# Soft shrinkage one slot sooner, and two extra frequency rows in another PSUM bank

## The chip, the cores and the metric

The kernel runs on one core of one Trainium2 chip. The time is the device time of one execution in microseconds (us), and the time of a kernel is the median over several runs. One execution of each kernel was recorded by the hardware profiler. The core's engines are PE (matrix multiply), PEld (its weight loads), DVE (vector), ACT (scalar activations), POOL (general SIMD) and SP (which issues most DMAs). They run side by side, each through its own queue in order, and wait for each other on semaphores.

## The reference

One block of a network on a single sequence of 4096 tokens with 640 features: an adaptive layer norm, a spectral mixer, another layer norm and a gated feed-forward layer.

```python
mod = (_silu(c) @ w_mod)            # six vectors of 640: sa, ca, ga, sb, cb, gb
h = _layernorm(x) * (1 + ca) + sa
x = x + ga * _A_ref(h, A_w1, A_b1, A_w2, A_b2)     # spectral mixer
h = _layernorm(x) * (1 + cb) + sb
x = x + gb * ((_silu(h @ w_gate) * (h @ w_up)) @ w_down)
```

The mixer takes a real Fourier transform over the 4096 tokens, giving 2049 complex frequencies. For each frequency the 640 features fall into 4 blocks of 160, and each block goes through a complex two-layer network: a first layer with a rectifier, a second layer with a bias. The outputs are then shrunk:

```python
lam = 0.01
mr = jnp.abs(or_) - lam
or_ = jnp.sign(or_) * mr * (mr > 0)        # the same for the imaginary part
```

An inverse transform brings the result back to tokens. Shrinking `v` is the same as `relu(v - lam) - relu(-v - lam)`, and the same as `v - clamp(v, -lam, lam)`; the kernel uses both forms.

## The kernel before

The kernel has two parts. The first does the layer norm, the forward transform, the two-layer network, the shrinkage and the first half of the inverse transform. The second finishes the inverse transform and does the feed-forward layer; its instructions are put in order by a planner that runs when the kernel is built, with estimated costs, and it knows nothing of the first part's order. In both parts the order of each engine's queue is the order of the program text; a tile framework adds the semaphore waits that the data and the buffers need.

The first part, around the change, works on 8 chunks (`ch`) of frequencies with 4 feature blocks (`b`) each, so 32 units, and runs through slots `p` from 0 to 31. `on(f, p)` calls `f(p // 4, p % 4)`. Slot p, from 4 to 28 (`LAST` is 28), emits in this order:

- `stage_l1(p)`: the first layer of unit p. Its matmuls (L727) write three PSUM tiles `pl`: two with the tag `p1`, a third (the remainder features) with the tag `p3`. ACT reads each of the first two twice (L744, L745), DVE forms a low half `h` from the results (L746), ACT and DVE read the third (L758, L759).
- `stage_b`: the forward transform of a block of the next chunk (PE L631), with its evacuation on ACT (L638) and DVE (L639).
- in some slots, sums that make the modulation vectors (a `pm` tile, with the tag `p3` in some of them), and copies of the remainder features (DVE L685).
- `tail_l1(p)`: the rectified remainder (ACT L768, DVE L769).
- in even slots `inverse(p - 6)`, which is `stage_i`: the inverse transform of one half of a chunk from four shrunk views (PE L841, narrow matmuls into four tiles `pi` with tags p2, p1, p1, p3; copied out by ACT at L844; sent to memory through POOL's queue at L849).
- `shrink_v(p - 4)`: the shrinkage of one tile `tt`. DVE clamps it (L826) and subtracts the clamp from it (L827).
- `stage_l2(p - 1)`: the second layer of unit p - 1 (PE L795) into two tiles `pc` with the tag `p2`; DVE adds the bias and writes into `tt` (L797). Chunk 4 has 258 frequencies instead of 256, so its four units have a third, small tile `pc` of 2 rows, with the tag `p1`; DVE empties it at L803.
- in slots up to 28, modulation work on DVE (L548, L550) and a folding of the last weight matrix on POOL (L592), each with its loads.

Each tag has two PSUM buffers that rotate, so a tile waits until the tile of the same tag two places earlier has been read.

A unit of shrinkage is one `tt` tile: `tts[ch, i % 2, i // 2]` for unit 4 ch + i. The index i // 2 says which half of the features it holds, and i % 2 which of the chunk's two groups of 128 frequencies. Each `tt` is filled by the second layer of two units, b = 0 and 1 for the first half, b = 2 and 3 for the second. So units 4 ch and 4 ch + 1 are complete at the end of slot 4 ch + 2, and units 4 ch + 2 and 4 ch + 3 at the end of slot 4 ch + 4. `stage_i(ch, 0)` reads units 4 ch and 4 ch + 1 in slot 4 ch + 6, and `stage_i(ch, 1)` the other two in slot 4 ch + 8.

Slots 29 to 31 are written out separately. There `stage_i` of chunk 6 comes sooner, in slots 29 and 30, and units 25 to 29 are shrunk in these slots. In slot 29 units 25 and 27 (`LAST - 3`, `LAST - 1`) go another way: ACT makes both rectified parts at the head of the slot (`shrink_parts`, L816 and L817), into spare tiles `xn00` and `xn01`, and DVE subtracts them later (`shrink`, L820): for unit 25 after `tail_l1`, for unit 27 after `stage_i(6, 0)` has been emitted. Unit 26 goes through `shrink_v` in between. `xn00` and `xn01` are used once more, at the start of the second part.

Of the kernel before, what the change touches and what calls it, by code (L numbers as in the profile page):

```python
# [6 lines left out]
F32 = mybir.dt.float32  # L7
F32R = mybir.dt.float32r
AF = mybir.ActivationFunctionType
OP = mybir.AluOpType  # L10
# [3 lines left out]
P = 128  # L14
D = 640
# [151 lines left out]
def body(tc, x, w1, b1, w2, b2, wg, wu, wd, c, wm, k_fa, k_tb, k_tx, k_bx, k_ga, k_ge, k_id, out, dbg=None):  # L167
    nc = tc.nc
    pe, act, dve, pool = nc.tensor, nc.scalar, nc.vector, nc.gpsimd
# [27 lines left out]
    with ExitStack() as top:  # L197
        low_p = top.enter_context(tc.tile_pool(name="low_p", bufs=1, reuse_waits="tile"))
        per = top.enter_context(tc.tile_pool(name="per", bufs=1))
        ps = top.enter_context(tc.tile_pool(name="ps", bufs=2, space=PSUM))  # L200
# [9 lines left out]
        nlam = per.tile([P, 1], F32, name="nlam")  # L210
# [21 lines left out]
        with ExitStack() as af:  # L232
# [288 lines left out]
            p2 = af.enter_context(tc.tile_pool(name="p2", bufs=1, side="right", reuse_waits="tile"))  # L521

            acc = p2.tile([P, D], F32, name="acc")
            xn00 = p2.tile([P, D], F32, name="xn00")
# [58 lines left out]
            LAST = NP - 4  # L583
# [63 lines left out]
            def evac_r(ch, b, part=None):  # L647
                if part != 1:
                    evac_rh(ch, b)
                if part != 0:  # L650
                    evac_rl(ch, b)
# [27 lines left out]
            def rem_high(ch):  # L679
                rt = rts[ch] = low_p.tile([P, 2, 2, 258], F32R, tag="wt", name=f"rt{ch}")  # L680
                act.activation(rt[:, 0, :, 0:256], pbs[ch, 4], AF.Identity, scale=ca1[:, 4:5])
# [10 lines left out]
            def rem_move(ch):  # L692
                NN = width(ch)
                nc.sync.dma_start(rzd[ch, :, :, 0:NN], f32(rts[ch].rearrange("p l i k -> p (l i) k")[:, :, 0:NN]))
# [78 lines left out]
            def stage_l2(ch, b, then=()):  # L773
                h0, h1, r2, _ = hss[ch, b]
                late = []
                de = slice(160 * (b % 2), 160 * (b % 2) + 160)
                for q in range(3 if ch == CE else 2):
                    fs = slice(128 * q, 128 * q + 128) if q < 2 else slice(256, 258)
                    M = 128 if q < 2 else 2
                    W = 320 if q < 2 else 160  # L780
                    if b % 2 == 0 and q < 2:
                        tts[ch, q, b // 2] = p2.tile([P, 2, 320], F32, tag=("tt", "tu")[ch % 2], bufs=4, name=f"tt{ch}_{q}_{b // 2}")
                    pc = ps.tile([P, 512], F32, tag="p2" if q < 2 else "p1", name=f"pc{ch}_{b}_{q}")
                    seq = [(h0[:, 0, fs], w2a[:, b, 0:W]), (h0[:, 1, fs], w2a[:, b, 0:W]),
                           (h0[:, 0, fs], w2a[:, b, 320:320 + W]),
                           (h1[:, 0, fs], w2b[:, b, 0:W]), (h1[:, 1, fs], w2b[:, b, 0:W]),
                           (h1[:, 0, fs], w2b[:, b, 320:320 + W]),
                           (r2[:, fs], w2c[:, b, 0:W]), (r2[:, fs], w2c[:, b, 320:320 + W])]
                    if (ch, b) == (0, 0):
                        late.append((pc, [seq[k] for k in (2, 5, 7)]))  # L790
                        for i, k in enumerate((0, 1, 3, 4, 6)):
                            mm(pc[:M, :W], *seq[k], start=(i == 0), stop=False)
                        continue
                    for i, (l, m) in enumerate(seq):
                        mm(pc[:M, :W], l, m, start=(i == 0), stop=(i == len(seq) - 1))  # L795
                    if q < 2:
                        dve.tensor_tensor(tts[ch, q, b // 2][:, :, de], pc[:, :320].rearrange("p (r e) -> p r e", r=2),  # L797
                                          b2t[:, :, b, :], op=OP.add)
                        if then:
                            then[q]()  # L800
                    else:

                        dve.tensor_tensor(tts[ch, 0, b // 2][0:1, 1, de], pc[0:1, :160], b2t[0:1, 0, b, :], op=OP.add)  # L803
                for q, (pc, seq) in enumerate(late):
                    for i, (l, m) in enumerate(seq):
                        mm(pc[:, :320], l, m, start=False, stop=(i == 2))
                    dve.tensor_tensor(tts[ch, q, b // 2][:, :, de], pc[:, :320].rearrange("p (r e) -> p r e", r=2),
                                      b2t[:, :, b, :], op=OP.add)

            cos = {}  # L810
            flat = lambda ch, i: tts[ch, i % 2, i // 2].rearrange("p r e -> p (r e)")

            cls = []

            def shrink_parts(ch, i, w):
                act.activation(w, flat(ch, i), AF.Relu, bias=nlam)  # L816
                act.activation(flat(ch, i), flat(ch, i), AF.Relu, bias=nlam, scale=-1.0)  # L817

            def shrink(ch, i, w):
                dve.tensor_tensor(flat(ch, i), w, flat(ch, i), op=OP.subtract)  # L820

            def shrink_v(ch, i):
                if not cls:
# [27 lines left out]
            on = lambda f, p, *a: f(p // 4, p % 4, *a) if 0 <= p < NP else None  # L851
# [25 lines left out]
            def load_first_rows(lo, hi, q, e=slice(0, D)):  # L877
                for k in range(2):
                    q.dma_start(cf[k][lo:hi, :, e], s2[lo:hi, 2 * k:2 * k + 2, e])
# [47 lines left out]
            for p in range(LAST + 1):  # L927
                ch, b = p // 4, p % 4
                if p == 0:
                    first_blocks()  # L930
                if p < 4:
                    for f, *a in mods.get(p, ()):
                        f(*a)
                    continue
                on(stage_l1, p)
                if b == 0:
                    todo = [(ch, 3)]
                else:
                    todo = [(ch + 1, 4)] * (b == 1) + [(ch + 1, b - 1)]
                todo = [q for q in todo if q[0] < NCH]  # L940
                for q in todo:
                    stage_b(*q)
                    if q[1] < 4:
                        evac_b(*q)
                if p == 4:
                    evac_r(1, 2)
                    evac_r(1, 3)
                for f, *a in sums.get(p, ()):
                    f(*a)
                if b == 1 and ch + 1 < NCH:  # L950
                    rem_high(ch + 1)
                on(tail_l1, p)
                if b == 1 and ch + 1 < NCH:
                    rem_low(ch + 1)
                    rem_move(ch + 1)
                if b == 2 and ch + 1 < NCH:
                    rem_read(ch + 1)
                inverse(p - 6)
                on(shrink_v, p - 4)
                on(stage_l2, p - 1)  # L960
                if b == 3 and 2 < ch + 2 < NCH:
                    load_g(ch + 2)
                    load_tb(ch + 2)
                for f, *a in mods.get(p, ()):
                    f(*a)
                if p == LAST - 4:
                    cf += [rp.tile([P, 2, D], F32, tag=tag, name=f"cf{tag}") for tag in ("rm", "rr")]
                    load_first_rows(rb + 16, rl, nc.sync)
                elif p == LAST - 1:
                    load_first_rows(0, rb - 16, nc.sync)  # L970
# [29 lines left out]


            for p in range(LAST + 1, NP):
                if p == LAST + 1:
                    on(shrink_parts, LAST - 3, xn00)
                    xn01 = p2.tile([P, D], F32, name="xn01")
                    on(shrink_parts, LAST - 1, xn01)
                elif p == LAST + 3:
                    on(shrink_v, LAST)
                    on(shrink_v, LAST + 1)
                on(stage_l1, p)  # L1010
                on(tail_l1, p)
                if p == LAST + 1:
                    on(shrink, LAST - 3, xn00)
                    on(shrink_v, LAST - 2)
                    load_first_rows(rb - 16, rb, nc.sync)
                elif p == LAST + 2:
                    load_first()
                    first_gate()
                for f, *a in sums.get(p, ()):
                    f(*a)  # L1020
                if p == LAST + 1:
                    stage_i(NCH - 2, 0)
                    on(shrink, LAST - 1, xn01)
                elif p == LAST + 2:
                    stage_i(NCH - 2, 1)
                    load_first_rows(rb, rb + 16, nc.sync)
                on(stage_l2, p - 1)
# [62 lines left out]
        if dbg == "afno":  # L1090
            with tc.tile_pool(name="dbg", bufs=2) as dp:
                for t in range(8):
                    w = dp.tile([P, 4, D], F32, name="w")
# [8 lines left out]
        with ExitStack() as ff:  # L1102
# [1312 lines left out]
            mv, rs, _ = fst[3]  # L2415
# [16 lines left out]
            flat = [(t, n) for t in range(NT) for n in range(NW)]  # L2432
# [5 lines left out]
            for t in range(NS):  # L2438
                for n in range(NW):
                    if sum_at(n) == t:  # L2440
                        a, b = sum_w(n)
# [77 lines left out]
```

## Time and profile before

| | before |
|---|---|
| median of 3 runs | 1437.59 us (1434.8 to 1439.29) |
| profiled execution, own time | 1436.97 us |
| its span | 1435.1 us |
| granted TensorE clock, mean | 0.996 |
| busy PE, PEld, DVE, ACT, POOL | 97%, 91%, 76%, 51%, 37% |
| L826 and L827, the pair of `shrink_v` | 30 each |
| L816, L817 and L820 | 2 each, between 263.0 and 272.7 us |
| L803, two-row tiles of chunk 4 | 4, between 186.3 and 209.3 us |
| PE stretch of the second part from 340 us | 1084.73 busy of 1095.10 us |

Times in the profile are us from the start of the span. A row of a timeline has the start, the length, the engine, the line, and the tiles written and read; `x3` means three instructions in one row, and a bracket at the end says how long the engine had been idle before and what ended that. A PSUM tile goes by its name here (`pl`, `pc`, `pi`) without its number. PE's `x` counts two records for each matmul in full float32, so one `stage_i` of 16 matmuls shows as x32. Slot 10 begins near 126.4 us, slot 18 near 183.1, slot 29 near 263.9.

### The profile page before, as it was taken

Reading aid. Unit: us, or ns where it says so; the run is one execution under the profiler, and the core shown is the slowest. Engines: PE = TensorE matmul, PEld = TensorE weight load, DVE = VectorE, ACT = ScalarE, POOL = GpSimd, SP = SyncE. Lnnn points to the kernel's source line nnn. Section 1 sums busy time; section 2 is a strip of 40 time slices with the busy share of each in tenths; the row PEclk is TensorE's granted clock in tenths of the full one; section 3 lists DMA queues with packets and bytes.
Section 4 is the critical chain, followed back from the end, with each engine's and each line's share of the span. In section 5 each row is a group of like instructions: output and inputs, shape, how many; then the busy total and the mean of one; then the engine's idle time right before and its main releaser. Section 6 shows DMA issues by size and latency. Waiting matters only on the chain.

```text
span 1435.1 us, 24392 instructions
## 1 busy us (share of the span) xinstructions
PE 1398.6 (97%) x8828; PEld 1312.8 (91%) x8828; DVE 1093.3 (76%) x1971; ACT 736.0 (51%) x1490; POOL 536.7 (37%) x640
## 2 busy tenths in 40 slices
PE   6899999989999999999999999999999999999999
PEld 2699989868989888999999999999999999999999
DVE  8888888669887788767878778888647768567775
ACT  7855545545545555545565556555435345245432
POOL 5300320144444444324244434434324555146533
PEclk9999999999999999999999999999999999999999
DMA  9966677548677988897887997778796666966652
GB/s 375 321 231 212 214 228 236 197 151 264 230 247 275 342 281 292 322 358 238 281 294 239 330 386 247 255 262 291 293 322 231 210 216 240 355 220 223 207 186 91
DMA packets 182794, 372.89 MB, mean 260 GB/s; under 512 B 21360, under 2 KB 103856, under 8 KB 180880
## 3 DMA queue, kind: packets, MB, share of 16 engines
q1 hardware_dynamic: 174624, 355.19, 71.5%
q0 software_dynamic: 6464, 13.50, 2.9%
q10 hardware_dynamic: 1584, 2.62, 0.5%
q8 instruction: 70, 1.15, 0.3%
q14 instruction: 52, 0.43, 0.1%
HBM read 266.40 MB, written 104.86 MB: 259 GB/s over the span
## 4 chain that ended last, share of the span: by engine, by line
PE 78%; DVE 12%; DMA 4%; ACT 2%; issue 2%; POOL 1%; SPq 0%; DVEq 0%; ACTq 0%; POOLq 0%
PE pd L2389 14%; PE pw L2070 8%; PE pw L2072 8%; PE pw L2071 8%; PE pd_X L2251 5%; PE pc L795 5%; PE pl L727 4%; PE pg L1935 3%; PE pg L1934 3%; PE pg L1936 3%; PE pd_Y L2251 3%; PE pw L2081 2%; PE pw L2083 2%; PE pw L2082 2%; DVE wb L1411 2%
## 5 line engine op out<-in xcount | busy, mean ns | idle before, releaser
L2389 PE MATMUL pd<-wdh,a 128*128 128x320 f32 x1040 | 239.1, 310 | 0.6 <-DVE x L2361 0.6
L2389 PEld LDWEIGHTS pd<-wdh,a 128*128 128x128 f32 x1040 | 176.2, 188 | 1.1 <-DVE x L2361 0.8
L2389 PE MATMUL pd<-wdl,a 128*128 128x320 f32 x540 | 166.2, 309 | 0.0
L1411 DVE TENSOR_TENSOR wb<-r,wb 128x512 fp32r<-128x512 f32 (+3 forms) x154 | 153.9, 1010 | 11.5 <-ACT wb L1408 10.1
L2070 PE MATMUL pw<-h,wt 128*128 128x384 f32 x416 | 141.2, 340 | 2.4 <-ACT s_x L2089 2.4
L2072 PE MATMUL pw<-h,wt 128*128 128x384 f32 x416 | 140.2, 337 | 0.0
L2071 PE MATMUL pw<-h,wt 128*128 128x384 f32 x416 | 139.9, 336 | 0.0
L2361 DVE TENSOR_TENSOR x<-x,pd 128x320 f32<-128x320 f32 x240 | 109.3, 478 | 37.0 <-PE pd L2389 32.8
L1408 ACT ACTIVATE wb<-r 128x512 fp32r<-128x512 f32 (+3 forms) x170 | 117.4, 703 | 33.9 <-PE pw L2083 25.2
L2070 PE MATMUL pw<-h,wb 128*128 128x384 f32 x312 | 105.0, 336 | 0.9 <-DVE x L2361 0.9
L2071 PE MATMUL pw<-h,wb 128*128 128x384 f32 x312 | 104.6, 335 | 0.0
L2072 PE MATMUL pw<-h,wb 128*128 128x384 f32 x312 | 104.6, 335 | 0.0
L1934 PE MATMUL pg<-ht,wb 128*128 128x512 f32 x260 | 102.3, 394 | 0.0
L1936 PE MATMUL pg<-ht,wb 128*128 128x512 f32 x260 | 101.4, 390 | 0.3 <-DVE wb L1411 0.3
L2389 PEld LDWEIGHTS pd<-wdl,a 128*128 128x128 f32 x540 | 101.4, 188 | 0.3
L1935 PE MATMUL pg<-ht,wb 128*128 128x512 f32 x260 | 101.4, 390 | 0.0
L2089 ACT ACTIVATE s_x<-pw 128x384 f32<-128x384 f32 x52 | 25.4, 489 | 120.3 <-PE pw L2072 119.4
L1639 POOL TENSOR_TENSOR cr<-cr,gab 128x640 f32<-128x640 f32 x28 | 46.9, 1678 | 98.1 <-DMA cr<-s 62.1
L2070 PEld LDWEIGHTS pw<-h,wt 128*128 128x128 f32 x416 | 78.1, 188 | 4.0 <-ACT s_x L2089 4.0
L2071 PEld LDWEIGHTS pw<-h,wt 128*128 128x128 f32 x416 | 78.2, 188 | 0.0
L2072 PEld LDWEIGHTS pw<-h,wt 128*128 128x128 f32 x416 | 78.1, 188 | 0.0
L2225 DVE TENSOR_TENSOR x<-x,pd_X 128x320 f32<-128x320 f32 x144 | 64.5, 484 | 14.2 <-PE pd_X L2251 14.2
(348 smaller groups left out, 3887.9 us busy)
## 6 DMA issues: line engine op xcount, KB each, us to landing
wt<-td SPq DMA_DIRECT2D x104, 512.0 KB, 5.3
hs<-ho SPq DMA_DIRECT2D x52, 512.0 KB, 5.8
h<-hs SPq DMA_DIRECT2D x32, 768.0 KB, 9.1
r<-in_B_w_up_dram SPq DMA_DIRECT2D x36, 640.0 KB, 5.1
r<-in_B_w_gate_dram SPq DMA_DIRECT2D x36, 640.0 KB, 5.1
wdr<-wdd SPq DMA_DIRECT2D x25, 640.0 KB, 5.6
td<-wt SPq DMA_DIRECT2D x25, 512.0 KB, 5.7
g<-s SPq DMA_DIRECT2D x7, 1280.0 KB, 7.2
```

The lines of the kernel that those rows point to most:

```text
L795: mm(pc[:M, :W], l, m, start=(i == 0), stop=(i == len(seq) - 1))
L1408: act.activation(wbs[t, n][:, 0, ks, e], raw[t, n][:, ks, e], AF.Copy)
L1411: (pool if onp else dve).tensor_tensor(wbs[t, n][:, 1, ks, e], raw[t, n][:, ks, e], f32(wbs[t, n][:, 0, ks, e]), op=OP.subtract)
L1934: mm(b, wh, hh, start=(kk == 0), stop=False)
L1935: mm(b, wh, hl, start=False, stop=False)
L1936: mm(b, wl, hh, start=False, stop=(kk == 4))
L2070: mm(b, w(0, kp), a[:, kp, 0], start=start and kp == 0, stop=False, skip_group_check=not start)
L2071: mm(b, w(0, kp), a[:, kp, 1], start=False, stop=False, skip_group_check=not start)
L2072: mm(b, w(1, kp), a[:, kp, 0], start=False, stop=kp == 1, skip_group_check=not start)
L2251: mm(bk[b, i][:, :320], x, y, start=new and j == 0, stop=j == len(seq) - 1, skip_group_check=not new)
L2361: dve.tensor_tensor(x2[:, e], x2[:, e], x[0][:, :320], op=OP.add)
L2389: mm(pd[g, hf][0][:, :320], l, m, start=i == 0, stop=i == len(s) - 1 and not (last and len(gs) > 1))
```

## The change

The shrinkage of a unit, which stood in slot unit + 4, stands in slot unit + 3 from slot 11 on. Slot 10, the eleventh, does two units, 6 and 7, so that none is left out. Slot 28 thus ends with unit 25 done, and slot 29 shrinks units 26 and 27, both with `shrink_v` on DVE. The way over ACT (`shrink_parts` and `shrink`) is gone, and `xn00` and `xn01` serve the second part alone. In the second layer, the third tile of chunk 4's units takes the tag `p3` instead of `p1`.

```diff
-                    pc = ps.tile([P, 512], F32, tag="p2" if q < 2 else "p1", name=f"pc{ch}_{b}_{q}")
+                    pc = ps.tile([P, 512], F32, tag="p2" if q < 2 else "p3", name=f"pc{ch}_{b}_{q}")
...
-            def shrink_parts(ch, i, w):
-                act.activation(w, flat(ch, i), AF.Relu, bias=nlam)
-                act.activation(flat(ch, i), flat(ch, i), AF.Relu, bias=nlam, scale=-1.0)
-
-            def shrink(ch, i, w):
-                dve.tensor_tensor(flat(ch, i), w, flat(ch, i), op=OP.subtract)
...
                 inverse(p - 6)
-                on(shrink_v, p - 4)
+                for q in [p - 4] if p < 10 else [6, 7] if p == 10 else [p - 3]:
+                    on(shrink_v, q)
                 on(stage_l2, p - 1)
...
             for p in range(LAST + 1, NP):
-                if p == LAST + 1:
-                    on(shrink_parts, LAST - 3, xn00)
-                    xn01 = p2.tile([P, D], F32, name="xn01")
-                    on(shrink_parts, LAST - 1, xn01)
-                elif p == LAST + 3:
+                if p == LAST + 3:
                     on(shrink_v, LAST)
                     on(shrink_v, LAST + 1)
                 on(stage_l1, p)
                 on(tail_l1, p)
                 if p == LAST + 1:
-                    on(shrink, LAST - 3, xn00)
+                    xn01 = p2.tile([P, D], F32, name="xn01")
                     on(shrink_v, LAST - 2)
+                    on(shrink_v, LAST - 1)
                     load_first_rows(rb - 16, rb, nc.sync)
...
                 if p == LAST + 1:
                     stage_i(NCH - 2, 0)
-                    on(shrink, LAST - 1, xn01)
```

## The prediction

> **What bounds the kernel now.** I read the page first (busy shares, and the profiled execution's own time, 1436.97 us, beside its span of 1435.1), then the waits of PE over the stretch that the change touches, then the timeline around each wait.
>
> ```profile
> span 1435.1 us, 24392 instructions
> PE 1398.6 (97%) x8828; PEld 1312.8 (91%) x8828; DVE 1093.3 (76%) x1971; ACT 736.0 (51%) x1490; POOL 536.7 (37%) x640
> ```
>
> PE is busy for 97% of the span, so work taken off DVE or ACT is worth only what it lets PE do sooner. The question is where PE stands still between 160 and 300 us, the second half of the spectral part.
>
> ```profile
> engine line waited for: us in total, times, longest us
> PE pl L727 <- DVE tt L803: 2.4, 1, 2.4
> PE pi L841 <- DVE tt L820: 1.9, 1, 1.9
> ...
> PE pc L795 <- ACT co L844: 0.3, 1, 0.3
> ```
>
> Two waits stand out, and the two edits meet exactly these. The first is for L803, the addition that empties the bank of the two additional rows; the second is for L820, the subtraction that ends a shrinkage begun on ACT. The timeline of the first (start, length, engine, line):
>
> ```profile
> 184.72 0.82 DVE L827 TENSOR_TENSOR tt<-tt,cl 128x640 f32<-128x640 f32 x1
> 185.46 0.88 DVE L797 TENSOR_TENSOR tt<-pc,b2t 128x320 f32<-128x320 f32 x2
> 186.26 0.30 DVE L803 TENSOR_TENSOR tt<-pc,b2t 1x160 f32<-1x160 f32 x1
> 186.61 0.62 PE L727 MATMUL pl<-z,w1a 128*128 128x258 f32 x3 [2.38 <-DVE tt L803]
> 189.24 1.33 PE L841 MATMUL pi<-tt,bx 32*64 32x320 f32 x32
> 190.63 1.43 ACT L844 ACTIVATE co<-pi 128x320 f32<-128x320 f32 x4
> ```
>
> DVE works without a gap here and is late. In p1 the thin tile takes the buffer that the second `pl` of the next slot wants, so PE waits for a 0.30 us instruction at the end of DVE's queue. The second place:
>
> ```profile
> 263.00 0.85 ACT L816 ACTIVATE xn<-tt,nlam 128x640 f32<-128x640 f32 x1
> 265.62 0.83 ACT L817 ACTIVATE tt<-tt,nlam 128x640 f32<-128x640 f32 x1
> 266.36 0.46 ACT L744 ACTIVATE h<-pl,b1m 128x256 f32<-128x256 f32 x1
> 267.66 1.06 PE L841 MATMUL pi<-tt,bx 32*64 32x320 f32 x8
> 269.31 0.42 DVE L769 SCALAR_TENSOR_TENSOR r<-u,r 64x256 fp32r<-64x256 f32 x1 [0.48 <-ACT r L768]
> 269.74 0.83 DVE L820 TENSOR_TENSOR tt<-xn,tt 128x640 f32<-128x640 f32 x1
> 270.62 2.41 PE L841 MATMUL pi<-tt,bx 32*64 32x320 f32 x24 [1.90 <-DVE tt L820]
> ```
>
> The inverse stage gets through its first quarter (x8 of x32, the unit already shrunk) and stops for unit 25, whose subtraction sits on DVE behind the low halves of the first layer; these wait for ACT, which first did four shrinkage activations. What that costs is more than 1.90 us, as the busy times by stretch show (first the stretch and its length, then PE's busy time and count; PEclk, the granted clock, is third from the end):
>
> ```profile
> 183.08:193.54 10.46, 8.08 (x89) 7.01 (x86) 8.70 (x17) 4.49 (x11) 0.52 (x1) 1.00 0.92 267
> 201.00:208.84 7.84, 7.84 (x88) 6.99 (x86) 5.89 (x13) 4.48 (x11) 1.94 (x4) 1.00 0.90 308
> 260.32:264.04 3.72, 3.72 (x50) 3.04 (x50) 3.27 (x6) 3.28 (x8) 1.37 (x3) 1.00 0.11 44
> 267.66:270.57 2.91, 1.06 (x9) 0.39 (x8) 2.13 (x5) 1.05 (x3) 0.00 (x0) 0.93 0.49 109
> 270.57:277.22 6.65, 6.60 (x41) 5.08 (x41) 2.52 (x5) 1.43 (x4) 0.00 (x0) 0.52 0.71 275
> 340.00:1435.10 1095.10, 1084.73 (x6460) 1050.87 (x6458) 820.89 (x1424) 534.79 (x1063) 449.96 (x488) 1.00 0.77 266
> ```
>
> **The change part by part. The bank.** Slot 18 (183.08 to 193.54) holds the same matmuls as slot 20 (201.00 to 208.84), and took 10.46 us against 7.84: 2.62 more, of which the wait is 2.38. With the thin tile in p3, p1 rotates only among tiles that ACT empties early. What is late next is p3: it has two buffers, and the fourth `pi` of slot 18 now takes the thin tile's. It would start 2.38 earlier than 189.24, at 186.86, and L803 ends at 186.56, so it fits by 0.3 us; DVE's queue up to there has no gap and no dependence on the wait, so L803 doesn't come later. Slot 18's four copies on ACT (190.63) come earlier too, but behind the low half of the remainder, and could hold the second `pc` by a tenth or so, as they do for 0.3 us in slot 22. Bounds: nothing (the wait reappears at p3) to 2.62; I take 2.3, near the wait's own row, because every instruction after it has its inputs.
>
> **The shrinkage, slots 10 to 28.** From slot 11 each slot does one pair L826, L827 at the same place in DVE's queue as before, on a unit written one slot later; the tile was written by DVE itself a slot earlier, so no wait is added, and no instruction or DMA moves past another queue. Only slot 10 gets a second pair. The DVE rows there and in the slot after, with PE's next second layer among them:
>
> ```profile
> 131.90 0.49 DVE L826 TENSOR_SCALAR cl<-tt 128x640 f32<-128x640 f32 x1
> 132.43 0.83 DVE L827 TENSOR_TENSOR tt<-tt,cl 128x640 f32<-128x640 f32 x1
> 133.18 1.08 DVE L797 TENSOR_TENSOR tt<-pc,b2t 128x320 f32<-128x320 f32 x2
> 135.65 0.43 DVE L746 TENSOR_TENSOR h<-h,h 128x256 fp32r<-128x256 f32 x1 [0.60 <-ACT h L745]
> 136.61 0.43 DVE L746 TENSOR_TENSOR h<-h,h 128x256 fp32r<-128x256 f32 x1 [0.53 <-ACT h L745]
> 136.88 0.69 PE L795 MATMUL pc<-w2a,h 128*128 128x320 f32 x3
> 137.89 0.75 DVE L639 SCALAR_TENSOR_TENSOR z<-pb,ca,z 128x512 fp32r<-128x512 f32 x1 [0.40 <-ACT z L638]
> ```
>
> The pair costs 0.49 + 0.83 = 1.32 us. Behind it queue L797 and the low halves; DVE idles 0.60, 0.53 and 0.40 in the next slot, 1.53 in all, which swallows it before L639. PE asks for the first bank that L797 empties at 136.88; L797 ends by 134.26 now and by 135.6 then. I cost the pair at 0; without that cover it is 1.32 once.
>
> **The shrinkage, slot 29.** Unit 25 is now done in slot 28, in the place that unit 24 had. ACT loses four activations (263.00 to 266.45, about 0.84 each); DVE loses two subtractions (0.83 and about as much) and gains a pair for unit 27, while the pair for 26 stays. So after the low halves (L769 ends at 269.73 now, and no later with ACT freed) DVE does two pairs, 2.64 us, before it empties slot 29's first `pc`, by some 273. PE asks for that bank in slot 30's inverse, a first layer of 21 matmuls after the slot's end:
>
> ```profile
> 277.38 2.50 PE pl L727 x21
> ```
>
> With the slot ending at 267.66 + 3.72 = 271.4 that is 273.9: hidden, by about 1 us, and if not, the price is DVE's lateness alone. Slot 28 ran the same two stages, inverse and second layer, in 3.72 us with the same count (x50); slot 29 took 2.91 + 6.65 = 9.56 us. With nothing to wait for it should take 3.72: 5.84 saved. Of this the granted clock of 0.52 is 6.65 x 0.48 = 3.2 us, the stop 2.6. Bounds: 1.9 (the stop alone as the waits give it, clock low anyway) to 5.84; I take 5.8, since the row of slot 28 is the same work.
>
> The Trainium skill, page "TensorE: Matmul & The Clock Gate", section on Part 1, the HAM clock gate, says that the clock falls to half after an idle window of about 3.4 us that runs free of the kernel, and its table of what matters for kernels asks only to avoid gaps of over some 3 us. The trace goes beyond that: the clock fell after a stop shorter than that, while the 2.38 us of the first place left it at 1.00. By a window that runs free the fall would be a matter of phase, so that other executions might not show it and the sum would lack 3.2 us; that is the second rival below.
>
> **Sum.** 2.3 + 5.8 = 8.1. Nothing behind gives it back by itself: after 340 us PE is busy 1084.73 of 1095.10 us in an order fixed when the kernel is built, so a start that is 8 us earlier passes to the end. 1436.97 - 8.1 = 1428.87 for such an execution; the median of the three runs, 1437.59, stands 0.62 above the profiled one, so **1429.5 us**.
>
> **The rivals.** (1) The first gain is given back, to p3 or to a transfer. PE's work of chunk 6 starts at slot 21 and needs its factors `tb`:
>
> ```profile
> 196.86 1.44 SPq L292 DMA_DIRECT2D tb<-in_k_tb_dram x1
> tb<-in_k_tb_dram SPq DMA_DIRECT2D x1, 256.0 KB, 10.2
> 211.38 1.95 PE L631 MATMUL pb<-tb,g 128*128 128x128 f32 x16
> ```
>
> They land at 196.86 + 10.2 = 207.1 and are wanted at 211.38, then at 209.1. For: the slack falls from 4.3 to 2.0, and p3's is 0.3. Against: both are still positive. Price 2.3: 1431.8.
>
> (2) The half clock is phase, not a consequence: only the stop goes. For: the 2.38 us wait left no mark on the clock. Against: the stop comes on top of narrow matmuls (1.06 us of busy time in 2.91 at 0.93), as one cause would look. Gain 2.3 + 2.6: 1432.7.
>
> (3) The early shrinkage doesn't free the inverse, since something else (a `pi` bank still being read by the ACT instruction that L816 held up) ends the wait too. Against: PE continues right when the L820 of 269.74 ends. Only the bank's 2.3 are left: 1435.3.
>
> (4) Slower: p3 is the worse rotation. In slots 18, 19 and 20 its next user (fourth `pi`, the modulation sum, fourth `pi`) waits for L803. DVE can be late by microseconds where POOL multiplies:
>
> ```profile
> 176.96 4.37 DVE L550 SCALAR_TENSOR_TENSOR acc<-wm,sc,acc 128x640 f32<-128x640 f32 x1
> 177.57 3.06 POOL L592 TENSOR_TENSOR wdf<-wdf,gbb 128x640 f32<-128x640 f32 x2
> 201.54 0.30 DVE L803 TENSOR_TENSOR tt<-pc,b2t 1x160 f32<-1x160 f32 x1
> 204.54 1.33 PE L841 MATMUL pi<-tt,bx 32*64 32x320 f32 x32
> ```
>
> If that happens ahead of an L803, PE stands within a stage of narrow matmuls, which in slot 29 cost 5.84 with the clock. Two such places cost 11.7, against a gain of 8.1: 1441.2. It decides when L803 is over 2.7 us later than in slot 20 now (201.84 against 204.54), over 0.3 in slot 18. Against: DVE had recovered by slot 20, and the long POOL stretch above lies ahead of the one L803 that was late already and still fits.
>
> **How the numbers follow.** Forecast 0.63; rival (1) 0.12, (2) 0.12, (3) 0.08, (4) 0.05. From no change a measurement here can tell about 0.3%, 4.3 us: faster means under 1433.3. The forecast lies 8 under; (1) and (2) lie 4.9 to 5.8 under and mostly count as faster, in a quarter of cases not, since three runs spread over 4.5 us; (3) is no change; (4) slower or none. So faster 0.81, same 0.15, slower 0.04. The range: at the low end the largest sum, 2.62 + 5.84 + 0.3 = 8.8, and some 2.5 us for the spread of runs, 1426.3; at the high end (1) and (2) with 2 us of the spread, 1434.5. About 0.15 is left out.
>
> **What would show it.** In the profile after, PE has no wait for L803 and none in the inverse of chunk 6; slot 18 takes about 7.9 us and slot 29's inverse with second layer about 3.7 at a granted clock of 1.00; L816, L817 and L820 are gone; L826 counts 32 instead of 30; the span is near 1427. Wrong would be: a wait of PE in slots 18 to 20 on a p3 tile (steps of the bank), a clock under 1 elsewhere before 320 us (rival 2, the gain moved), a DVE that is late in slots 11 or 30 (the cover), or the end not moving though 340 us comes 8 earlier.

## The result, and the profile after

The changed kernel took **1431.65 us** (median of 6 runs, 1428.65 to 1432.22), against 1437.65 for the kernel before (6 runs, 1434.8 to 1443.37). The ratio is 0.9949, with a 95% interval of 0.9928 to 0.9969: faster by some 7.3 us (4.5 to 10.4); the two medians differ by 6.0. Gains in this text come from the ratios and can differ from those of the medians by 1 us or a little more. Two more comparisons of the same two kernels, among the experiments below, gave 0.9964 and 0.9957, or 5.2 and 6.2 us. The forecast was 8.1 us, and 1429.5 as a time.

The profiled execution took 1432.05 us. The head of its page:

```profile
span 1430.2 us, 24392 instructions
PE 1397.4 (98%) x8828; PEld 1312.4 (92%) x8828; DVE 1094.6 (77%) x1973; ACT 731.8 (51%) x1486; POOL 536.7 (38%) x640
```

ACT has four instructions fewer and is busy 4.2 us less, DVE has two more. PE has the same 8828, which now take 1397.4 us of busy time instead of 1398.6. The waits of PE between 160 and 300 us:

```profile
engine line waited for: us in total, times, longest us
PE py L1038 <- PE pc L795: 0.8, 1, 0.8
PE py L1038 <- DVE tt L820: 0.4, 1, 0.4
PE pc L795 <- ACT co L837: 0.3, 1, 0.3
```

Both waits that the edits aim at are gone. (Lines have moved: the pair of `shrink_v` is now L819 and L820, the inverse matmul L834, its copy L837, and the forward transform of the two additional frequencies, `px`, L855.) The timeline of the changed kernel at both places, slot 18 first, then slot 29:

```profile
186.62 0.52 PE L727 MATMUL pl<-z,w1a 128*128 128x258 f32 x3
187.27 0.82 DVE L820 TENSOR_TENSOR tt<-tt,cl 128x640 f32<-128x640 f32 x1
188.01 0.88 DVE L797 TENSOR_TENSOR tt<-pc,b2t 128x320 f32<-128x320 f32 x2
188.81 0.30 DVE L803 TENSOR_TENSOR tt<-pc,b2t 1x160 f32<-1x160 f32 x1
189.18 1.33 PE L834 MATMUL pi<-tt,bx 32*64 32x320 f32 x32
...
267.77 1.33 PE L834 MATMUL pi<-tt,bx 32*64 32x320 f32 x32
269.03 0.71 PE L795 MATMUL pc<-w2a,h 128*128 128x320 f32 x3
271.71 0.88 DVE L797 TENSOR_TENSOR tt<-pc,b2t 128x320 f32<-128x320 f32 x2
274.06 1.79 PE L834 MATMUL pi<-tt,bx 32*64 32x320 f32 x32
```

In slot 18 the second `pl` no longer waits, though L803 is as late on DVE as it was. L803 ends at 189.11, and the inverse, whose fourth tile takes that buffer, starts at 189.18. In slot 29 the 32 records of the inverse run through in one row. DVE empties slot 29's second layer by 272.59, and slot 30's inverse asks for the buffer at 274.06. By stretch (slot 18, slot 29's inverse with second layer, slot 12, and the second part; the granted clock is third from the end):

```profile
185.63:193.67 8.04, 8.04 (x89) 7.00 (x86) 7.89 (x16) 4.46 (x11) 0.00 (x0) 1.00 0.97 279
267.76:271.50 3.74, 3.74 (x50) 3.06 (x50) 3.14 (x6) 1.84 (x5) 0.00 (x0) 1.00 0.44 89
141.17:150.04 8.87, 8.44 (x89) 7.59 (x88) 7.20 (x15) 4.47 (x11) 2.40 (x5) 1.00 0.57 218
340.00:1430.20 1090.20, 1080.19 (x6431) 1046.36 (x6429) 816.33 (x1417) 530.07 (x1056) 447.80 (x486) 1.00 0.77 266
```

Slot 18 takes 8.04 us instead of 10.46, and the stretch in slot 29 takes 3.74 instead of 9.56. That is 8.24 us, near the predicted 8.1. Yet this span is only 4.9 shorter than the one before. A table of all profiles says where the rest is. Each slot runs from PE's first L727 of it to that of the next; "head" is the start of slot 10, "rest" runs from the start of slot 31 to the end, and the slots left out are the same everywhere within 0.1 us.

| profile | head | slot 12 | slot 18 | slots 19 to 24 | slots 25 to 28 | slot 29 | rest |
|---|---|---|---|---|---|---|---|
| before | 126.38 | 8.19 | 10.46 | 43.74 | 26.76 | 13.18 | 1151.11 |
| before again (e4) | 126.34 | 8.19 | 12.00 | 43.73 | 26.75 | 11.82 | 1153.60 |
| after | 128.25 | 8.87 | 8.04 | 43.72 | 26.75 | 7.34 | 1151.96 |
| after again (e3) | 124.71 | 8.41 | 8.03 | 43.71 | 26.75 | 7.34 | 1152.46 |
| after, third (e8) | 125.01 | 8.59 | 8.04 | 43.73 | 26.75 | 7.34 | 1152.97 |
| bank only (e1) | 125.73 | 8.18 | 8.00 | 43.71 | 26.76 | 12.76 | 1152.64 |
| shrinkage only (e2) | 126.65 | 11.86 | 12.02 | 43.75 | 26.76 | 7.33 | 1153.06 |
| pair alone (e6) | 125.67 | 8.52 | 12.03 | 43.87 | 26.75 | 11.81 | 1152.99 |
| load ahead (e7) | 126.07 | 8.18 | 8.01 | 43.72 | 26.75 | 7.34 | 1153.65 |
| load ahead again (e12) | 127.44 | 8.18 | 8.00 | 43.73 | 26.75 | 7.34 | 1152.98 |
| pair in slot 25 (e5) | 126.92 | 8.19 | 8.04 | 43.72 | 27.61 | 7.34 | 1151.82 |
| pair in slot 21 (e11) | 126.64 | 8.18 | 8.05 | 45.12 | 26.75 | 7.34 | 1153.04 |
| stop filled (e9) | 126.27 | 8.18 | 10.46 | 43.75 | 26.75 | 10.36 | 1152.84 |
| DVE in place (e10) | 126.36 | 9.17 | 12.02 | 43.75 | 26.75 | 9.94 | 1154.45 |

From before to after: head +1.87, slot 12 +0.68, slot 18 -2.42, slot 29 -5.84, rest +0.85, together -4.86. Head and rest vary by 3.5 and 3.3 us over the profiles. The changed kernel's three heads alone range from 124.71 to 128.25, although the head lies ahead of everything that the change touches, and its rests (mean 1152.46) are those of the kernel before (mean 1152.36). These two columns are the spread of executions, and one thing in "rest" can be named. In all three profiles of the changed kernel the clock is at half for 3.41 us near 310 us (from 309.85, 306.26 and 306.99), close to the end of a stop of 2.0 us that both kernels have there. The stretch ahead of the fall and the fall itself, in the changed kernel's first profile:

```profile
306.44:309.85 3.41, 1.27 (x7) 0.59 (x5) 0.46 (x1) 2.05 (x3) 3.31 (x6) 1.00 0.54 192
309.86:313.26 3.40, 3.12 (x7) 2.51 (x8) 2.63 (x4) 3.40 (x7) 1.50 (x3) 0.50 0.74 218
```

The kernel before has such a fall in its second profile (from 317.23) and none in its first. Half of 3.41 us is 1.7, an estimate of what one fall can cost. Slot 12 is another matter.

### The profile page after: what moved, and what is told of

It is laid out like the page before. It is cut to its first block, busy times and chain, and to the rows that moved or that the text cites. A ratio compares the mean times of both kernels' runs of the same rounds, so it can differ in the third digit from the quotient of the medians.

```text
span 1430.2 us, 24392 instructions
## 1 busy us (share of the span) xinstructions
PE 1397.4 (98%) x8828; PEld 1312.4 (92%) x8828; DVE 1094.6 (77%) x1973; ACT 731.8 (51%) x1486; POOL 536.7 (38%) x640
## 3 DMA queue, kind: packets, MB, share of 16 engines
q10 hardware_dynamic: 1584, 2.62, 0.5%
## 4 chain that ended last, share of the span: by engine, by line
PE 80%; DVE 9%; DMA 5%; ACT 2%; issue 2%; POOL 1%; SPq 0%; ACTq 0%; DVEq 0%; POOLq 0%
PE pd L2379 14%; PE pw L2060 8%; PE pw L2062 8%; PE pw L2061 8%; PE pc L795 5%; PE pd_X L2241 5%; PE pl L727 4%; PE pg L1925 3%; PE pg L1924 3%; PE pg L1926 3%; PE pd_Y L2241 3%; PE pw L2071 2%; PE pw L2073 2%; PE pw L2072 2%; PE pb L631 2%
```

## The experiments

**One edit at a time (e1, e2), and both kernels again (e3, e4).** Bank only is the kernel before with this line; shrinkage only is the changed kernel without it.

```diff
-                    pc = ps.tile([P, 512], F32, tag="p2" if q < 2 else "p1", name=f"pc{ch}_{b}_{q}")
+                    pc = ps.tile([P, 512], F32, tag="p2" if q < 2 else "p3", name=f"pc{ch}_{b}_{q}")
```

> The kernel before with the third tile of chunk 4's units in p3, nothing else. Theory (both gains are real and add): PE's wait for L803 is gone, slot 18 takes 7.9 us instead of 10.46, slot 29 still stops and takes 9.5 at half clock; time 2.5 us under before. Rival (p3 holds PE instead, and only the earlier shrinkage let the inverse of slot 18 start at once): slot 18 keeps 9 us or more, with a wait of its inverse; time within 1 us of before.

> The change without the bank: shrinkage a slot sooner, the two-row tiles stay in p1. Theory: slot 18 keeps its 10.46 us with the wait of 2.4 for L803, slot 29's inverse and second layer take 3.7 us at full clock instead of 9.56; time 5.8 us under before. Rival (the earlier shrinkage costs DVE time elsewhere): under 4.5 us, with a wait of PE in slots 10 to 28 that before has not.

> The changed kernel once more, for its head. In its first profile slot 10 began 1.9 us later than in that of before, and the forward step of slot 12 waited 0.7 us for a load, ahead of anything that the change touches. Theory (that is what executions differ by): slot 10 begins between 125.5 and 129 us here, not tied to the kernel, and the time is 8 us under before by the medians, give or take 1.5. Rival (the change itself delays the head by 1.9 to 2.5 us): slot 10 begins past 128 us here and before 127 in the kernel before and in the bank alone; time 6 us under before.

> The kernel before once more, for its head and for the clock in slot 29. Theory: time within 1 us of before; slot 10 begins between 125.5 and 129 us; the granted clock after the stop of slot 29 is near 0.5 again, since the stop comes on top of narrow matmuls. Rival (the half clock is a matter of phase): here, or in the bank alone, slot 29 takes about 6.4 us at a clock of 1.00.

| kernel | median, us | ratio to before (1437.99) | 95% interval |
|---|---|---|---|
| e1, bank only | 1434.7 | 0.9978 | 0.9968 to 0.9987 |
| e2, shrinkage only | 1434.86 | 0.9983 | 0.9973 to 0.9994 |
| e3, after again | 1432.1 | 0.9964 | 0.9951 to 0.9977 |
| e4, before again | 1437.56 | 0.9997 | 0.9988 to 1.0006 |

Of e3's expectations neither was met in full: slot 10 began at 124.71, earlier than either range, so the change doesn't delay the head, but the gain of 5.2 is nearer to the rival's 6 than to 8. In e4 the clock fell in slot 29 again, though for less time than before.

The bank is worth 3.2 us (1.9 to 4.6), the shrinkage 2.4 (0.9 to 3.9), and both together 5.2 (3.3 to 7.0), so the two add up within these intervals. The bank pays at least what was expected of it, and the shrinkage less than half of its 5.8, with a wait of PE that before has not, as the rival to it had said. The shrinkage's profile has slot 29 as short as in the changed kernel (7.33), so the loss is elsewhere. The waits of PE between 120 and 290 us in shrinkage only name the place:

```profile
engine line waited for: us in total, times, longest us
PE pl L727 <- DVE tt L803: 2.4, 1, 2.4
PE px L855 <- DMA g<-s: 1.9, 1, 1.9
PE pc L795 <- ACT co L837: 0.3, 1, 0.3
```

The second row is new. The kernel before has no wait for a load of `g` there; the changed one has a small one. The rows that lead to it, first in the kernel before (DVE's modulation sum, SP's issues, PE's use of `g`):

```profile
134.18 0.88 DVE L550 SCALAR_TENSOR_TENSOR acc<-wm,sc,acc 128x640 f32<-128x640 f32 x1
135.08 0.35 SPq L543 DMA_DIRECT2D wm<-in_w_mod_dram  x1
135.47 0.62 SPq L304 DMA_DIRECT2D g<-s  x1
142.68 1.18 PE L862 MATMUL px<-tx,g 128*128 128x2 f32 x10
```

The same four in the changed kernel:

```profile
137.23 0.88 DVE L550 SCALAR_TENSOR_TENSOR acc<-wm,sc,acc 128x640 f32<-128x640 f32 x1
138.14 0.35 SPq L543 DMA_DIRECT2D wm<-in_w_mod_dram  x1
138.53 0.62 SPq L304 DMA_DIRECT2D g<-s  x1
145.14 1.25 PE L855 MATMUL px<-tx,g 128*128 128x2 f32 x10 [0.43 <-DMA g<-s]
```

The load of a piece of the modulation weight (L543) overwrites the buffer that L550 reads, and is issued 0.02 us after L550 ends in the one and 0.03 in the other. Behind it in SP's queue stands the load of chunk 4's `g` (L304). The pair added in slot 10 stands ahead of L550 in DVE's queue. From slot 10's start (126.38 and 128.25), L550 begins at 7.80 before and 8.98 after, and `g` is issued at 9.09 before and 10.28 after: 1.19 later. The trace's list of DMAs has the same row in both kernels (KB, then us from issue to landing) and says how long `g` takes:

```profile
g<-s SPq DMA_DIRECT2D x1, 1280.0 KB, 6.5
```

So `g` landed at 141.97 before, 0.71 ahead of its use at 142.68. A delay of 1.19 uses that up and leaves 0.48; PE waited 0.43. The slot is 0.68 longer; 0.16 of that is because the `px` record no longer begins before the record ahead of it ends. In shrinkage only the load took 8.0 us, and PE waited 1.91; the clock then fell to half. Its timeline, and the stretch after it, of which 3.41 us are at half clock:

```profile
136.94 0.62 SPq L304 DMA_DIRECT2D g<-s  x1
145.03 1.25 PE L855 MATMUL px<-tx,g 128*128 128x2 f32 x10 [1.91 <-DMA g<-s]
...
147.00:151.44 4.44, 4.44 (x32) 3.75 (x17) 1.94 (x4) 1.43 (x4) 2.78 (x6) 0.62 0.39 148
```

The slot took 11.86 us instead of 8.19. The kernel before, profiled again, shows something else too. Its slot 18 has the same stop of 2.4 us, but this time the clock fell after it, while in slot 29 the mean over the stretch is higher than in the first profile (0.67 instead of 0.52):

```profile
186.57:190.50 3.93, 3.93 (x21) 3.83 (x21) 1.96 (x4) 1.22 (x3) 0.00 (x0) 0.62 1.00 256
272.10:277.34 5.24, 5.23 (x40) 4.12 (x41) 2.48 (x5) 1.43 (x4) 0.00 (x0) 0.67 0.90 342
```

The bank's stop is therefore worth 2.4 us in one execution and 4.0 (12.00 - 8.03) in another.

Figures such as 0.62 and 0.67 are means over a stretch. Cut finer, the clock of all 14 profiles is 1.00 or 0.50 and nothing between, and, the very end of the span apart, it stays at half for 3.41 us or twice that (slot 29: 6.83 us in the first profile of before, 3.41 in the second). The falls of one profile lie on a grid: in the second profile of before they begin at 187.52, 272.86 and 317.23, which are 25 and 13 times 3.413 us apart. What differs between executions is how a stop lies on this grid. Slot 18's stop of 2.38 us, by the grid stretch that holds most of it, first in the second profile and then in the first (PE's busy time comes first behind the length, the clock third from the end):

```profile
184.11:187.52 3.41, 1.03 (x9) 0.95 (x9) 3.38 (x8) 0.84 (x2) 0.00 (x0) 1.00 1.00 323
184.83:188.24 3.41, 1.63 (x13) 1.63 (x14) 2.86 (x6) 0.37 (x2) 0.00 (x0) 1.00 0.99 286
```

In the second profile the stop lies whole in one stretch, and the clock falls at its end, 187.52. In the first it is split, and the clock stays. From 60 us on, and short of the last 4 us, take the grid stretches of the 14 profiles that ran at full clock. All 23 in which PE was busy for less than 1.53 us were followed by the half clock, 8 of 31 between 1.53 and 2.17, and 1 of 5511 above. This was read from the traces afterwards; no run shifts a stop against the grid.

**The extra pair by itself (e6).** The kernel before, with a second pair of the same size in slot 10. Its result goes to a tile that nothing reads, so it is added work.

```diff
                 on(shrink_v, p - 4)
+                if p == 10:
+                    dve.tensor_scalar(cls[0], flat(1, 3), LAM, -LAM, op0=OP.min, op1=OP.max)
+                    dve.tensor_tensor(xn00, flat(1, 3), cls[0], op=OP.subtract)
```

> The kernel before with one more clamp and subtraction of the same size on DVE in slot 10, into a spare tile that nobody reads; nothing else. New theory: the load of chunk 4's first tile is issued 1.2 us later after the start of slot 10 (10.3 instead of 9.1 us), slot 12 takes 8.4 to 11.9 us instead of 8.2, and the time is 0.2 to 3.7 over before, 1.5 by the medians. By the prediction's step (hidden): slot 12 at 8.2, time as before.

Median 1438.32 against 1437.73, ratio 1.0011 (1.0000 to 1.0022): slower by 1.6 us (the medians differ by 0.6), at the edge of what can be told from nothing. In its profile `g` is issued 10.29 us after slot 10's start, as late as in the changed kernel. It took 6.1 us to land this time, and slot 12 took 8.52 instead of 8.19.

**The pair elsewhere (e5, e11).** The changed kernel, with the step forward made in another slot: slots 11 to 20, or 11 to 24, keep the old order, and slot 21 or slot 25 does two units.

```diff
-                for q in [p - 4] if p < 10 else [6, 7] if p == 10 else [p - 3]:
+                for q in [p - 4] if p < 25 else [21, 22] if p == 25 else [p - 3]:
```

and for slot 21:

```diff
-                for q in [p - 4] if p < 10 else [6, 7] if p == 10 else [p - 3]:
+                for q in [p - 4] if p < 21 else [17, 18] if p == 21 else [p - 3]:
```

> The change, with the doubled shrinkage in slot 25 (units 21 and 22) instead of slot 10; slots 10 to 24 shrink as before, slot 29 as in the change. New theory (in slot 10 the second pair holds the modulation addition, that holds the next load of a modulation row in SP's queue, and behind this the load of chunk 4's first tile, which slot 12 then waits for): slot 12 takes 8.2 us again, slots 18 and 29 stay at 7.9 and 7.3; time 1 to 2.5 us under the changed kernel, 8 under before. Rival (slot 12's wait is what loads differ by anyhow): slot 12 waits here too, time as in the changed kernel.

> The change with the doubled shrinkage in slot 21 (units 17 and 18), where DVE is some 5 us behind, instead of slot 10. Theory (a pair costs nothing only where DVE has idle time before PE asks for its banks): slot 12 at 8.2 us, but PE waits for the bank of slot 22's inverse, so that slots 19 to 24 take 1.2 to 4.5 us more than their 43.7; time as in the changed kernel or up to 3 us over it. Rival (a pair is hidden anywhere, only SP's queue matters): slots 19 to 24 at 43.7, time as with the load ahead.

With slot 25: 1430.67, ratio 0.9948 (0.9935 to 0.9961), beside 0.9957 (0.9945 to 0.9969) for the changed kernel on the same chip (e8, below), whose median is only 0.25 us longer; the 1 us or more that was expected between them isn't shown. With slot 21: 1432.64, ratio 0.9963 (0.9948 to 0.9977). In both, slot 12 is back at 8.19 and 8.18, and another slot pays. DVE's rows and the inverse that they hold up, in the timeline of the pair in slot 21:

```profile
217.01 0.83 DVE L820 TENSOR_TENSOR tt<-tt,cl 128x640 f32<-128x640 f32 x1
217.75 0.88 DVE L797 TENSOR_TENSOR tt<-pc,b2t 128x320 f32<-128x320 f32 x2
218.29 1.34 PE L834 MATMUL pi<-tt,bx 32*64 32x320 f32 x32 [1.38 <-DVE tt L797]
```

The inverse takes the buffer that L797 empties, and L797 stands behind the pair. The pair's 1.32 us shows in full as a wait of 1.38, and slots 19 to 24 take 45.12 us instead of 43.72. With slot 25 the same row is there, smaller:

```profile
245.77 1.34 PE L834 MATMUL pi<-tt,bx 32*64 32x320 f32 x32 [0.20 <-DVE tt L797]
```

The second layer behind it waits 0.30 for ACT's copies, and slots 25 to 28 take 27.61 instead of 26.75 there. The pair thus costs 0.2 to 0.7 us in slot 10 of the changed kernel's profiles, 0.86 in slot 25 and 1.40 in slot 21. By the profiles it is free in none of the three; times can't tell 0.2 to 0.9 us from nothing.

**The load ahead of the one that waits (e7, e12), and the changed kernel a third time (e8).** The changed kernel, where chunk 4's `g` and `tb` are issued in slot 10, ahead of its modulation load, instead of in slot 11, behind it. All else is as it was.

```diff
-                if b == 3 and 2 < ch + 2 < NCH:
+                if p == 10:
+                    load_g(4)
+                    load_tb(4)
+                if b == 3 and 4 < ch + 2 < NCH or p == 7:
```

> The change with the pair left in slot 10, and chunk 4's two loads issued in slot 10 ahead of the modulation row instead of in slot 11. New theory: slot 12 at 8.2 us though the pair is where it was, time 1 to 2.5 us under the changed kernel. Rival (DVE's lateness reaches PE some other way): slot 12 keeps its wait.

> The changed kernel a third time, to stand beside the others of this call. New theory: slot 12 between 8.4 and 11.9 us; time 6 us under before.

> The change with chunk 4's loads issued in slot 10 ahead of the modulation row, a second time. Theory: slot 12 at 8.2, slot 18 at 8.0, slot 29 at 7.3 us; time 7 to 8.5 us under before, which is 1 to 2.5 under the changed kernel.

| kernel | median, us | ratio to before | 95% interval |
|---|---|---|---|
| e7, load ahead | 1429.26 | 0.9945 | 0.9933 to 0.9957 |
| e8, after, third | 1430.92 | 0.9957 | 0.9945 to 0.9969 |
| e12, load ahead again | 1429.0 | 0.9935 | 0.9924 to 0.9947 |

Timeline of the first of them:

```profile
133.24 0.62 SPq L304 DMA_DIRECT2D g<-s  x1
142.37 1.18 PE L855 MATMUL px<-tx,g 128*128 128x2 f32 x10
```

`g` is issued 7.17 us after slot 10's start (126.07), took 6.8 us by the trace's list of DMAs, and lies ready 2.3 us before its use. Slot 12 takes 8.18 in both, with the pair still in slot 10. So the pair's price there is the load's place in SP's queue. This version gains 7.9 and 9.3 us over the kernel before, 8.6 on average. The changed kernel's three comparisons average 6.2. The intervals of e7 and e8, timed side by side, overlap, so that it beats the changed kernel too, by some 2.4 us, is likely and not certain; both its medians are the lowest of the kernels timed beside it. Nor need all of the 2.4 be the pair's: a slow load can make slot 12 late without the pair (e10, below), and no run puts the load ahead in the kernel before.

**The stop in slot 29, filled (e9), and made without ACT (e10).** e9 is the kernel before with 13 matmuls into an unused tile between slot 29's first layer and its inverse. e10 is the kernel before with ACT's four shrinkage activations gone; `shrink_v` does the two units at the places in DVE's queue where the subtractions stood.

```diff
+                    idle(13)
                     stage_i(NCH - 2, 0)
```

> The kernel before, with 13 dummy matmuls of 128 x 128 ahead of slot 29's inverse stage, into a PSUM tile that nobody reads, so that PE works through the 2.9 us in which it stood still. Theory (the clock falls because PE stands still there): the clock stays at 1.00 and slot 29 takes 3.6 + 2.9 + 3.7 = 10.2 us instead of 11.8 to 13.2; time 1.5 to 3 us under before. Rival (the clock falls by itself there): slot 29 at 11.8 or more.

```diff
-                    on(shrink_parts, LAST - 3, xn00)
...
-                    on(shrink_parts, LAST - 1, xn01)
...
-                    on(shrink, LAST - 3, xn00)
+                    on(shrink_v, LAST - 3)
...
-                    on(shrink, LAST - 1, xn01)
+                    on(shrink_v, LAST - 1)
```

> The kernel before, with units 25 and 27 shrunk by the DVE pair at the place where their subtractions stood in slot 29; ACT's four activations are gone, no unit moves to another slot, the bank stays. Theory (PE waits because DVE does unit 25 behind the low halves, ACT only adds some tenths): slot 29 still stops for over 2 us and takes 11.3 to 12.8 us. Rival (ACT's four activations were what held PE): slot 29 takes 7.4 to 8.5 us.

e9: 1436.49 against 1437.64, ratio 0.9994 (0.9983 to 1.0005). Its stretches in slot 29, the added matmuls first, then inverse and second layer:

```profile
267.49:270.57 3.08, 3.08 (x29) 2.96 (x28) 2.28 (x6) 1.12 (x3) 0.00 (x0) 1.00 0.22 59
270.57:274.29 3.72, 3.72 (x50) 3.05 (x49) 2.42 (x5) 1.43 (x4) 0.00 (x0) 1.00 0.99 339
```

The inverse begins at 270.57, since unit 25 isn't ready sooner than before, but now PE works until then. The clock stays at 1.00, and the same 50 records take 3.72 us. Slot 29 takes 10.36 us instead of the 11.8 to 13.2 of the four other profiles in which ACT begins the shrinkage and PE stops. One profile without a fall would prove little, as e10 shows; but in none of the eight profiles whose slot 29 has no stop, nor of the eight whose slot 18 has none, does the clock fall there. So the half clock comes with the stop, and not by itself. The timed gain, 0.9 us with an interval from a gain of 2.4 to a loss of 0.7, is below the 1.5 to 3 that were expected and can't be told from none.

e10: 1438.25, ratio 1.0000 (0.9988 to 1.0013). Timeline and stretches of its slot 29:

```profile
272.80 1.31 PE L841 MATMUL pi<-tt,bx 32*64 32x320 f32 x24 [1.86 <-DVE tt L827]
...
270.18:273.00 2.82, 0.96 (x17) 0.40 (x24) 2.26 (x5) 0.42 (x1) 0.00 (x0) 1.00 0.54 113
273.00:276.50 3.50, 3.50 (x41) 2.81 (x32) 2.95 (x6) 1.43 (x4) 0.00 (x0) 1.00 0.88 356
```

Neither expectation was met. ACT's activations are gone and the stop is still 1.86 us long, so DVE's order makes it: unit 25 is done behind the low halves, whichever engine begins it. ACT's four did delay the low halves: L769 ends 5.69 us after the slot's start before and 4.83 in e10; but unit 25's pair is 0.5 us longer than its subtraction was. The clock did not fall, and the slot took 9.94 us, between the two forecasts. A stop of the same length thus passed without the half clock in this execution; the grid stretch that holds it (270.43 to 273.84) has PE busy for 1.55 us. Its slot 12 took 9.17 with no pair in slot 10: `g` was issued at 9.10 after the slot's start and needed 8.0 us to land, 1.5 more than before, which is more than the slack of 0.71.

## Why the prediction was right, step by step

**The bank: right.** 2.3 us was forecast, 2.42 shows in the profile, and the timed 3.2 (1.9 to 4.6) agrees with it. The upper bound of 2.62 took slot 20 for the same work; without the wait slot 18 takes 8.04 and slot 20 7.83. If the timed gain is really above 2.4, the clock would explain it, which the first profile showed at 1.00 through the 2.38 us wait: in four of the six profiles that still have this wait (e2, e4, e6, e10) slot 18 took 12.0 us, and in two (before, e9) 10.46. "It fits by 0.3" held with 0.07: L803 ends at 189.11, the inverse starts at 189.18.

**Slot 29: right in mechanism, sized to one execution.** The inverse and second layer take 3.74 us at a clock of 1.00, where 3.72 was forecast. The gain of 5.84 belongs to the execution that was profiled. Against the second profile of before it is 4.5 (11.82 - 7.34), against DVE in place 2.6 (9.94 - 7.34). That the sum of both places comes to 8.3 us in the first profile and 8.4 in the second is luck: in the first the clock fell in slot 29 for twice as long and not at all in slot 18. "Hidden, by about 1 us" was 1.47 (272.59 to 274.06).

**Rival (2), phase, was half right.** In slots 18 and 29 the clock does not fall without a stop, so the fall is a consequence and went with the stop, against the rival. But whether it falls goes with the phase, as the rival had it, that is, with how the stop lies on the grid: in executions of the same kernel slot 18's stop was followed by no fall or one of 3.41 us, slot 29's by one of 3.41 or 6.83. The Trainium skill, page "TensorE: Matmul & The Clock Gate", section on Part 1, says that the window is "free-running", so that where in it the work lands varies from run to run; the grid of 3.413 us in the traces agrees. That page's table of what matters for kernels asks to avoid gaps of over some 3 us, and here stops of 1.9 and 2.4 us were enough: the measurement decides. The prediction also named a clock under 1 elsewhere before 320 us as a sign of being wrong, and the changed kernel shows it, near 310 us. It lies at a stop that both kernels have and that the change does not touch, and the kernel before shows it in one of two profiles, so it may be phase as well. All seven profiles with both edits have it and three of the other seven; whether the change makes it more frequent stays open.

**Slot 10: the step that failed.** The prediction cost the extra pair at 0. "No instruction or DMA moves past another queue" was said of the slots from 11 on; for slot 10 it held that DVE's idle 1.53 us would swallow the pair before L639, and looked at PE's banks alone. DVE does catch up: L639 begins 11.51 us after slot 10's start in both kernels. But L550 lies ahead of the idle time, it frees the buffer for SP's next load, and chunk 4's `g` stands behind that load in SP's queue with 0.71 us to spare. Price: 0.22 to 0.68 us in the changed kernel's three profiles, 1.6 (0.0 to 3.2) by the pair alone, and 3.67 in the profile where the clock fell after the wait. All four rows that give it (L550, L543, L304, the use of `g`) were in the trace of before. With the load moved ahead, the change gains 8.6 us on average, close to the sum of 8.1; as made, 6.2. The missed term is thus of the right size for the gap between sum and measurement, but that it is all of the gap isn't shown.

**Nothing behind gives it back: held.** The rest of the kernel, 1151 to 1154 us, shows no difference between the two kernels beyond the spread of executions. Rivals (1), (3) and (4) did not happen: no wait for `tb`, slot 29 free, no wait on a p3 tile in slots 18 to 20. A transfer did take some of the gain, as rival (1) has it, but another one, six slots earlier.

**Open.** How often the wait in slot 12 trips the clock in executions without a profile, and so whether the 2.4 us between the changed kernel and the one with the load ahead are slot 12 alone: its profiles show only 0.2 to 0.7. The mean granted clock of the timed runs of the experiments and of the result gives a hint: 0.9956 over 66 runs of the kernel before, 0.9970 over 17 of the changed one, 0.9979 over 11 with the load ahead. Times 1433 us that is 6.3, 4.3 and 3.0 us of lost clock, so by this estimate some 2 us of the 6.2 gained are clock, where the prediction had 3.2 of 8.1, and about half of the 2.4. Why filling the stop gained 0.9 us timed where its profile shows more stays open too. Two profiles of the kernel before are too few to give the mean cost of its stops.

## What to carry to other kernels

When an instruction is added to one engine, follow the buffers that the instructions behind it free, into the DMA queue: a load that waits for such a buffer holds every load queued behind it, and the slack to look up is that of the last of these. Here the remedy was to issue the load that is wanted soon ahead of the one that waits. And a stop of PE that is priced from one profiled execution, with the clock that this one happened to have, can be off by more than half: the same stop cost 2.4 or 4.0 us in slot 18, and 4.5 or 5.8 in slot 29.

## What was not expected of the hardware

- The same stop gives different clocks: slot 18's 2.38 us left the clock at 1.00 in one execution of the kernel before and halved it for 3.41 us in another, 10.46 against 12.00 us for the slot. Slot 29's stop halved it for 6.83 us, for 3.41 and, in e10, not at all. The falls of a profile lie whole multiples of 3.413 us apart. Each stretch of this grid with PE busy for less than 1.53 us was followed by a fall; slot 18's stop, where it was split over two stretches with more, was followed by none.
- One load of 1280 KB, issued behind the same load of the same queue, took from 6.0 to 8.0 us to land (6.0 in e3, 6.5 in before, 8.0 in e2 and e10). The slack of 0.71 us is smaller than this spread, so slot 12 can be late without any change.
- The time from the start of the span to slot 10, where all kernels compared here run the same instructions, ranged from 124.71 to 128.25 us. A difference of 3 us between two spans says nothing until it is found in a slot.
